# Transposes by DMA, row sums inside the value matmuls, and a reordered start, in a kernel of sparse attention and two dense layers

## The chip, the cores and the metric

The kernel runs on one core of one Trainium2 chip. The metric is the time of one execution on the device in microseconds (us). Engines: PE is the matmul engine, PEld its weight loads, DVE the vector engine, ACT the scalar engine, POOL the engine that issues the software DMA queue, SP the one that issues stores and, after the change, transposes.

## The reference, cut to what matters

```python
# q, k, v: (8 batches, 8 heads, 576, 64) fp32;  w_in: 512 x 2048, w_out: 2048 x 512
scores = (1/sqrt(64)) * q @ k.T
mask_local   = (rel >= 0) & (rel < 32)                 # heads 0..3, rel = pos_q - pos_k
mask_strided = (rel >= 0) & (pos_k % 32 == pos_q % 32) # heads 4..7
attn = softmax(where(mask, scores, -1e9));  o = attn @ v
x = o.transpose(0, 2, 1, 3).reshape(8 * 576, 512)
h = x @ w_in
g = where(h > 0, h, exp(min(h, 0)) - 1)
out = g @ w_out
```

Per core that is 8 batches of 4 pairs of heads (two strided, two local), and two dense layers of 4608 x 512 x 2048. The dense layers are most of the work. The inputs q and k have a standard deviation of 0.1, so all scores are near zero; this comes back in the first experiment.

## The kernel before: the parts that the change touches

All inputs come in by the software DMA queue, which casts fp32 to bf16 on the way. A score matmul wants the head dimension on the partitions, so q and k are transposed on PE, into PSUM, and copied back by DVE. A row sum comes from a matmul with a block of ones; sums and values of two heads are put side by side as two 64-column tiles.

```python
def load_str(src, b, name):                  # strided heads of q, k or v
    t = p_in.tile([RS, HG, NS * D], BF16, tag=name, name=name)
    nc.gpsimd.dma_start(out=t, in_=src[b, HG:2*HG].rearrange("h (p s) d -> p h (s d)", s=NS))
# load_batch(b): qs, ks, vs (strided), then ql, kl, vl (local), all on nc.gpsimd

def piece_T(P):                              # transposes of one pair of heads
    for nm, dst in (("q", P.qT[:, 0:S]), ("k", P.kT[:, PRE:PRE + S])):
        ps = p_a.tile([128, S], BF16, tag="a", name="tp")
        ... nc.tensor.transpose(ps[:, o:o + RS], src[...], identity[0:RS, 0:RS])   # 8, or 6
        nc.vector.tensor_copy(dst, ps)

def piece_O(P, u, pm):                       # half a pair: sums, values, division
    ... nc.tensor.matmul(s_ps[x*D:(x+1)*D, :], lhsT=ones, rhs=pm[:, x], ...)       # x = 0, 1
    ... nc.tensor.matmul(o_ps[x*D:(x+1)*D, o:o+RS], lhsT=batch_in[P.b]["vs"][...], ...)
    ln = Ln(s_ps); rc = Exp(-ln)             # ACT, 128 x 288 each
    ... nc.vector.tensor_mul(dst, o_ps, rc)  # DVE, 128 x 288

def l1(nb, m):                               # 4 matmuls of 512 columns, one hidden block
    hps = p_h.tile([128, CHUNK], F32, tag="h")
    for c in range(KC): nc.tensor.matmul(hps, lhsT=w_in_sb[:, cc, m*128:(m+1)*128], ...)
    e = Exp(hps)                             # ACT
    e1 = min(e, 1) - 1;  g = max(e1, hps)    # DVE, two operations

while done < PB:                             # all of batch 0's attention first
    run_piece(pieces[done], ...); done += 1
for nb in range(NCH):
    for m in range(MC):
        if nb > 0: l2(nb - 1, m)             # 4 matmuls of 512 columns
        run_piece(pieces[done]); done += 1   # the next batch's attention, T of it first
        l1(nb, m)
```

The softmax here doesn't subtract the row's maximum and nothing guards it: scores larger than these inputs give would overflow.

## Time and profile before

| | before |
|---|---|
| time, median of the first 3 runs (range) | 362.08 us (359.04 to 363.35) |
| span of the profiled run | 361.1 us |
| first layer-1 matmul | 36.32 us |
| PE waiting for strided q and k, in all | 22.0 us |

A table of waits has the waiting engine with tile and line, what released it, then the sum in us, how often, and the longest. These two rows of the kernel before are the 22.0 us:

```profile
PE tp L203 <- DMA qs<-in_q_dram: 18.4, 3, 9.4
PE tp L203 <- DMA ks<-in_k_dram: 3.6, 3, 1.4
```

Both are waits of the transposes for their input, three times each, the last of them at 62 us. In the prediction you will see them again as single holes, in a view where each line is a stretch of like instructions: start, busy time, engine, line, output and inputs, weight and moving shapes, count, and in brackets the idle time before it. Busy times there contain pipeline drain; what a piece costs is the distance between starts.

### The profile page before, as it was taken

The page shows a single profiled execution, that of the slowest core. Times are in us where ns is not written, and L with a number is a line of the kernel's source. Part 1 is how long each engine was busy: PE and PEld are TensorE (multiplying, and loading weights), DVE is VectorE, ACT ScalarE, POOL GpSimd, SP SyncE. Part 2 cuts the span into 40 slices and gives each one's busy share as a digit, 9 for nine tenths or more (in the row PEclk, how much of TensorE's full clock was granted, in tenths as well). Part 3 has the DMA queues.
Part 4 walks back from the last instruction along what each step waited for, and adds up shares of the span by engine and source line. Part 5 has one row for each costly group of instructions (what it writes and reads, how often), then busy time and mean ns, then how long its engine had stood idle before and what let it go on. Part 6 is the DMA issues. An engine that isn't in the chain of part 4 may idle for free.

```text
span 361.1 us, 6843 instructions
## 1 busy us (share of the span) xinstructions
PE 329.1 (91%) x2656; PEld 161.5 (45%) x2656; DVE 243.8 (68%) x501; ACT 194.3 (54%) x377; POOL 92.3 (26%) x120
## 2 busy tenths in 40 slices
PE   1851986999999999999999999999999999999995
PEld 1630443454544544445454454444444444444442
DVE  2640797787877877777878777776666666666610
ACT  1650575667566666666666666664444433543411
POOL 7952843958507214510620000000000000000000
PEclk9999999899999999999999999999999999999999
DMA  6999999999959965992960111010111110021122
GB/s 91 113 178 178 107 199 158 99 159 152 142 93 102 96 101 72 87 114 63 119 48 29 31 31 31 29 32 29 46 44 30 34 55 29 29 59 31 30 71 76
DMA packets 88321, 29.03 MB, mean 80 GB/s; under 512 B 72672, under 2 KB 83680, under 8 KB 88288
## 3 DMA queue, kind: packets, MB, share of 16 engines
q0 software_dynamic: 82432, 19.14, 61.7%
q1 hardware_dynamic: 5856, 9.44, 9.1%
q8 instruction: 21, 0.34, 0.4%
q14 instruction: 12, 0.10, 0.1%
HBM read 38.21 MB, written 9.44 MB: 132 GB/s over the span
## 4 chain that ended last, share of the span: by engine, by line
PE 73%; DMA 12%; ACT 6%; POOL 4%; issue 2%; DVE 2%; ACTq 0%
PE ops L382 32%; PE hps L347 30%; DMA vs<-in_v_dram 5%; DMA ks<-in_k_dram 5%; PE tp L211 3%; PE tp L203 2%; PE sc L243 2%; ACT e L251 2%; ACT osb L387 2%; DMA vl<-in_v_dram 2%; DVE pm L259 2%; PE s_ps L286 1%; ACT ln L297 1%; PE s_ps L270 1%; POOL kl L85 1%
## 5 line engine op out<-in xcount | busy, mean ns | idle before, releaser
L347 PE MATMUL hps<-xT,w_in_sb 128*128 128x512 bf16 x576 | 151.4, 386 | 0.2
L382 PE MATMUL ops<-w_out_sb,g 128*128 128x512 bf16 x576 | 145.4, 379 | 0.0
L352 ACT ACTIVATE he<-hps 128x512 f32<-128x512 f32 x144 | 85.8, 596 | 103.7 <-PE hps L347 103.0
L382 PEld LDWEIGHTS <-g 128*128 128x128 bf16 x576 | 56.4, 98 | 68.0
L347 PEld LDWEIGHTS <-w_in_sb 128*128 128x128 bf16 x576 | 50.8, 99 | 53.3 <-issue 2.1
L251 ACT ACTIVATE e<-sc 72x576 bf16<-72x576 f32 (+1 forms) x60 | 38.3, 639 | 17.4 <-PE sc L243 17.4
L297 ACT ACTIVATE ln<-s_ps 128x288 f32<-128x288 f32 x64 | 26.3, 411 | 16.9 <-PE s_ps L270 8.7
L387 ACT COPY osb<-ops 128x512 f32<-128x512 f32 x36 | 21.1, 586 | 20.0 <-PE ops L382 20.0
L76 POOL DMA_DIRECT2D ql<-in_q_dram x32 | 27.2, 855 | 18.0 <-PE tp L211 6.6
L299 ACT ACTIVATE rc<-ln 128x288 f32<-128x288 f32 x64 | 28.4, 443 | 2.0
L85 POOL DMA_DIRECT2D kl<-in_k_dram x32 | 23.7, 758 | 19.7 <-DMA ks<-in_k_dram 5.5
L203 PE MATMUL tp<-identity,qs 72*128 72x72 bf16 x128 | 7.9, 213 | 18.4 <-DMA qs<-in_q_dram 18.4
L304 DVE TENSOR_TENSOR xT<-o_ps,rc 128x288 bf16<-128x288 f32 x32 | 14.6, 456 | 8.3 <-ACT rc L299 7.9
L309 DVE TENSOR_TENSOR xT<-o_ps,rc 128x288 bf16<-128x288 f32 x32 | 14.6, 457 | 7.8 <-ACT rc L299 5.0
L253 DVE TENSOR_TENSOR pm<-e,mask_s 72x576 bf16<-72x576 bf16 x32 | 14.5, 452 | 3.8 <-ACT e L251 2.4
L259 DVE TENSOR_TENSOR pm<-e,mask_l 128x576 bf16<-128x576 bf16 x32 | 14.6, 457 | 2.5 <-ACT e L251 0.5
L203 PEld LDWEIGHTS <-qs 72*128 72x128 bf16 x128 | 5.8, 108 | 19.9 <-DMA qs<-in_q_dram 18.7
L67 POOL DMA_DIRECT2D vs<-in_v_dram x8 | 5.7, 710 | 31.9 <-PE sc L243 31.6
L96 POOL DMA_DIRECT2D vl<-in_v_dram x8 | 9.6, 1197 | 11.8 <-PE tp L203 11.4
L286 PE MATMUL s_ps<-pm,ones 128*64 128x288 bf16 x64 | 10.6, 322 | 1.6 <-DVE pm L259 0.9
L203 PE MATMUL tp<-identity,ks 72*128 72x72 bf16 x128 | 7.9, 214 | 3.9 <-DMA ks<-in_k_dram 3.6
L291 PE MATMUL o_ps<-pm,vl 128*64 128x96 bf16 x192 | 10.6, 215 | 0.7 <-DMA vl<-in_v_dram 0.7
(343 smaller groups left out, 338.5 us busy)
## 6 DMA issues: line engine op xcount, KB each, us to landing
out_dram<-osb SPq DMA_DIRECT2D x32, 144.0 KB
qs<-in_q_dram POOLq DMA_DIRECT2D x8, 288.0 KB, 5.9
ks<-in_k_dram POOLq DMA_DIRECT2D x8, 288.0 KB, 7.7
vs<-in_v_dram POOLq DMA_DIRECT2D x8, 288.0 KB, 7.9
ql<-in_q_dram POOLq DMA_DIRECT2D x32, 72.0 KB, 6.3
kl<-in_k_dram POOLq DMA_DIRECT2D x32, 72.0 KB, 4.2
vl<-in_v_dram POOLq DMA_DIRECT2D x8, 288.0 KB, 5.5
w_in_sb<-in_moe_w_in_dram POOLq DMA_DIRECT2D x4, 512.0 KB, 10.9
```

Source lines behind the costliest of these rows:

```text
L76: nc.gpsimd.dma_start(out=t[:, h // 2, :, h % 2, :], in_=q[b, h].rearrange("(p s) d -> p s d", s=NS))
L85: nc.gpsimd.dma_start(out=t[:, h // 2, :, h % 2, :], in_=src[b, h].rearrange("(t p) d -> p t d", p=LQ))
L203: nc.tensor.transpose(ps[:, o:o + RS], src[:, P.g0 + x, 2 * sp * D:2 * (sp + 1) * D], identity[0:RS, 0:RS])
L251: nc.scalar.activation(e[0:R], sc[0:R, :, 0:W], ACT.Exp, scale=scale)
L259: nc.vector.tensor_mul(pm, e, mb.unsqueeze(1).to_broadcast([128, 2, W]))
L297: nc.scalar.activation(ln, s_ps, ACT.Ln)
L299: nc.scalar.activation(rc, ln, ACT.Exp, scale=-1.0)
L304: nc.vector.tensor_mul(dst, o_ps.rearrange(pat, z=2, sp=2), rc.rearrange(pat, z=2, sp=2))
L347: nc.tensor.matmul(hps, lhsT=w_in_sb[:, cc, m * 128:(m + 1) * 128], rhs=xT[:, cc, nb * CHUNK:(nb + 1) * CHUNK], start=(c == 0), stop=(c == ...
L352: nc.scalar.activation(e, hps, ACT.Exp)
L382: nc.tensor.matmul(ops, lhsT=g[:, m, kk * 128:(kk + 1) * 128], rhs=w_out_sb[:, m, :], start=(m == 0), stop=(m == MC - 1))
L387: nc.scalar.copy(o_sb, ops)
```

## The change

The intent is to take the transposes and the separate row sums off PE, so that beside the dense layers only scores and values stay on it, and to start the dense layers earlier. Cut to its core:

```diff
+ def dma_T(b, which):                       # batches 2..7: all of q or k of a batch at once
+     nc.sync.dma_start_transpose(out=out_.rearrange("p (c n) -> p c n", n=n), in_=in_)
  def piece_O(b, hp, u, pm):                 # batches 3..7
-     s_ps by ones matmuls, o_ps by two 64-column tiles
+     for x, c, vt, mv in pv_terms(b, hp, u, pm):   # vt: 128 columns, values beside ones
+         nc.tensor.matmul(o[x][:, c], lhsT=vt, rhs=mv, ...)
-     ln = Ln(s_ps);  rc = Exp(-ln);  x = o_ps * rc                    # 128 partitions
+     ln[lo] = Ln(o[0][hi]);  ln[hi] = Ln(o[1][lo]);  rc = Exp(-ln)    # two halves
+     x_out(lo, o[0], rc);  x_out(hi, o[1], rc)
...
- t0["ql"] = load_qloc(0); t0["kl"] = load_kloc(k, 0, "kl")            # casting software queue
+ load_ql(0, nc.scalar, 0); load_kl(0, nc.sync, 0)                     # plain fp32
+ load_ql(0, nc.sync, 1);   load_kl(0, nc.scalar, 1)
+ cast_q(nc.vector, 0); cast_k(nc.scalar, 0); ...                      # bf16 by DVE and ACT
...
- def l1(nb, m):  4 matmuls of 512 columns
+ def l1(j, t):   8 matmuls of 256 columns, two hidden blocks
+ def l1_wide(j, t):                         # batch 0: four blocks of 256, a 4 KB PSUM tile
+     Exp and Relu on ACT, one DVE operation per 1024 columns
...
+ spins(26); ... f12 ...                     # filler matmuls between batch 0's pieces
+ for h in range(2):                         # layer 1 of tokens 0..511 ahead of batch 1
+     for j in range(2):
+         l1_wide(j, 4 * h)
+         if h: piece_T(1, 2 + j)            # batch 1 still transposes on PE
+         l1(j, 4 * h + 2); l1(j, 4 * h + 3)
...
+     at(st - (5 if b == 3 else 4), lambda b=b: Ts(b, "qs", "ks"))
+     at(st - (2 if b == 3 else 4), lambda b=b: Ts(b, "kl", "ql"))
...
+ def l2_last(j, kk): two halves, copied by ACT and DVE, stored by two queues
```

The bf16 tiles of local q and k, of the values that have ones beside them and of all transposed tensors exist twice, so one batch is loaded while another is used. In `at(n, ...)` the time n counts layer-1 groups; `st` is the step of a batch's first scores. Transposes stand 4 steps ahead of them; for batch 3 the strided two stand 5 ahead and the local two 2.

## The prediction

> **What bounds the kernel now.** I read the page first: the span, the busy line, the 40 slices.
>
> ```profile
> span 361.1 us, 6843 instructions
> PE 329.1 (91%) x2656; PEld 161.5 (45%) x2656; DVE 243.8 (68%) x501; ACT 194.3 (54%) x377; POOL 92.3 (26%) x120
> ...
> PE   1851986999999999999999999999999999999995
> ...
> DMA  6999999999959965992960111010111110021122
> ```
>
> PE is in the nines from slice 7 (about 62 us) to the end. Before that it has holes, and there the DMA row is full. So there are two stages: a start that waits for data, then a stage in which PE never rests. The windows view says so in numbers (columns: window, length, busy us of PE, PEld, DVE, ACT, POOL, clock, DMA share, GB/s):
>
> ```profile
> 20.00:30.00 10.00, 3.16 (x41) 2.02 (x41) 2.90 (x7) 4.03 (x10) 3.85 (x5) 1.00 1.23 202
> 30.00:40.00 10.00, 4.81 (x32) 2.22 (x33) 2.01 (x3) 1.13 (x2) 4.38 (x6) 1.00 2.27 141
> ...
> 100.00:150.00 50.00, 49.80 (x474) 24.55 (x471) 39.74 (x83) 33.85 (x68) 17.20 (x22) 1.00 0.85 94
> ```
>
> From 100 to 150 us PE is busy 49.8 of 50, DVE 39.7, ACT 33.9. The PE timeline of the start names the hole:
>
> ```profile
> 23.92 0.45 PE L291 MATMUL o_ps<-pm,vl 128*64 128x96 bf16 x6
> 33.78 0.66 PE L203 MATMUL tp<-identity,qs 72*128 72x72 bf16 x8 [9.42 <-DMA qs<-in_q_dram]
> 35.85 0.66 PE L203 MATMUL tp<-identity,ks 72*128 72x72 bf16 x8 [1.41 <-DMA ks<-in_k_dram]
> 36.32 1.90 PE L347 MATMUL hps<-xT,w_in_sb 128*128 128x512 bf16 x4
> ...
> 60.55 0.43 PE L203 MATMUL tp<-identity,qs 72*128 72x72 bf16 x8 [2.43 <-DMA qs<-in_q_dram]
> 61.80 0.66 PE L203 MATMUL tp<-identity,ks 72*128 72x72 bf16 x8 [0.82 <-DMA ks<-in_k_dram]
> 62.27 1.90 PE L347 MATMUL hps<-xT,w_in_sb 128*128 128x512 bf16 x4
> ```
>
> Batch 0's attention ends at 24.4 us; the first layer-1 matmuls start only at 36.3, because the program puts batch 1's transposes ahead of them. After 62.27 there is no hole.
>
> For the price of each piece I subtract start times in the steady PE timeline (its busy column includes pipeline drain):
>
> ```profile
> 150.36 0.31 PE L286 MATMUL s_ps<-pm,ones 128*64 128x288 bf16 x2
> 150.48 0.32 PE L291 MATMUL o_ps<-pm,vl 128*64 128x96 bf16 x6
> 150.73 0.43 PE L203 MATMUL tp<-identity,qs 72*128 72x72 bf16 x8
> 151.17 0.42 PE L203 MATMUL tp<-identity,ks 72*128 72x72 bf16 x8
> 151.43 1.03 PE L347 MATMUL hps<-xT,w_in_sb 128*128 128x512 bf16 x4
> 152.29 1.03 PE L382 MATMUL ops<-w_out_sb,g 128*128 128x512 bf16 x4
> 153.25 0.30 PE L243 MATMUL sc<-qT_95,kT_92 64*128 64x72 bf16 x8
> 153.49 1.04 PE L347 MATMUL hps<-xT,w_in_sb 128*128 128x512 bf16 x4
> ```
>
> The output piece (sums and values) is 150.73 - 150.36 = 0.37; the transposes 151.43 - 150.73 = 0.70, whose first eight take 0.44 and the next eight, of equal size, 0.26, so about 0.18 is a switch; four layer matmuls 0.86; the scores 0.24; and a layer-2 group that is followed by attention takes 0.96 rather than 0.86, so entering attention costs 0.10. One pair of heads is T + 2 S + 2 O + three entries = 0.70 + 0.48 + 0.75 + 0.30 = 2.23 us, 8.9 for a batch. The chain gives an independent count: equal places of two successive batches start 29.84 us apart (81.95, 111.79, 141.63); less 12 steps of 1.73 for the two layers that leaves 9.1. I use 9.1. PE's whole load is then 1152 layer matmuls x 0.216 = 249 plus 8 x 9.1 = 73, or 322 us; the other 39 us are the start and a tail of 4 us (the last output copy starts at 357.07).
>
> **What the Trainium skill says.** "TensorE: Matmul & The Clock Gate", under "Wait — 56ns, not 53.3ns?": a warm matmul of N columns costs N/2.4 ns plus about 2.5. The trace agrees: 0.865/4 = 216 ns at N = 512. For N = 256 that gives an estimate of 109 ns, so twice as many half-size layer-1 matmuls cost 576 x 2.5 ns = 1.4 us more. The same page, under "What you observe" and "What's actually happening", has an idle array fall to half clock: after the 9.4 us hole four matmuls took 1.90 instead of 1.03, so the trace agrees, and the filler matmuls of the change are meant for this. "SBUF — State Buffer", section "Door 1: The DMA port swizzle" (note on cachelines): 16-byte lines, full rate with two hits or more per line. The new layer-1 weights are read at a step of four bf16, 8 bytes, just two hits. No run here shows it yet. "DMA: Bandwidth & Descriptors", "Latency and other measured facts": a DMA transpose moves some 261 GB/s. A batch has 3 x 327,680 + 294,912 = 1.28 MB, an estimate of 5 us per batch, hidden if right; this trace has no such transfer.
>
> **The change part by part.**
>
> (1) Crossbar transposes for batches 2 to 7. Off PE go 24 pairs x 0.70 = 16.8 us, and 48 copies of 0.45 us off DVE.
>
> (2) For batches 3 to 7 the row sums come out of the value matmuls (ones beside the values as 128-column weights). O falls from 0.37 to 8 x 72 / 2400 = 0.24: 40 x 0.13 = 5.2 us. Without column tiling the entry into O should be nearly free too: some of 0.10 x 40, I take 2. My count per batch is 4 x (0.48 + 0.48 + 0.19) = 4.6 for batches 3 to 7, and 6.6 for batch 2, which keeps the old O and enters four times per pair: 4 x (0.48 + 0.76 + 0.40). PE load after: 249 + 1.4 + 2 x 9.1 + 6.6 + 5 x 4.6 = 298, that is 24 less.
>
> (3) DVE and ACT pay for (2): two half-partition multiplies and two logs in place of one each, 40 x 0.456 = 18 us on DVE and 40 x 0.411 = 16 on ACT. For batches 3 to 7 a batch has 16 layer-1 steps, 16 layer-2 steps and 4 pairs: 32 x 0.865 + 4.6 = 32.3 us of PE. DVE: 16 x (0.43 + 0.69) + 8 x 0.457 + 16 x 0.456 = 28.9. ACT: 16 x 0.596 + 8 x 0.64 + 16 x 0.411 + 8 x 0.443 + 4 x 0.586 = 27.1. Both stay below PE, at 89% and 84%.
>
> (4) The start. Batch 0's local q and k come as plain fp32 on the hardware queues and are cast by DVE and ACT; the software queue is left to the strided heads, v and w_in. Layer 1 of batch 0 now comes ahead of anything of batch 1. Two things must be ready: ACT has some 18 us of work for batch 0 (8 x 0.64 + 8 x 0.85, plus copies and casts), from about 5 us, so attention ends near 23; and w_in. Before, the same bytes had landed near 32 us. The transfers now start 3 to 4 us earlier, with q in 2 KB rows, so I put the first half of w_in at 24 and the second at 29. Layer 1 thus starts near 24 instead of 36.3. Later, w_out and batch 1 (before: landed near 57) bind: I expect 52 to 56, with PE waiting 3 to 8 us in all.
>
> (5) The end: the last outputs leave in half tiles on two engines and two queues: 4.1 us becomes about 3.5.
>
> Sum: 24 + (298 - 9 for batch 0) + 3.5 = 316.5 without a hole; with 3.5 us of waiting, **320 us**. Against 362 that is 12 us from the earlier start of layer 1, 24 from less PE work, and the rest small.
>
> **The rivals.**
>
> A. The start stays bound by transfers. For: its DMA row is full, and batch 1 and w_out still need the same bytes. Against: 16 layer-1 steps' worth of work needs only batch 0 and w_in. If batch 1 is complete only at 62, the time is near 328 to 332.
>
> B. Short strided weight loads are not hidden in layer 1. For: one load per 109 ns instead of per 216. Against: eight transposes with a weight load each took 0.26, or 33 ns a load. If 10 ns showed on each, 1152 x 10 ns = 12 us: 332.
>
> C. DVE or ACT becomes the bound at 85 to 90%, or crossbar transposes hold up the output stores on the same SP queue until three output buffers are full. For: the loads in (3). Against: four transposes at 5 us per 32 us, and buffers for three tiles. Either would add 5 to 20 us.
>
> D. The start runs better than I think (layer 1 at 20, no hole afterwards): 311.
>
> **Range and chances.** 320 lies between D and A/B; each single failure costs about 10, so 310 to 332 should hold it 8 times in 10. To lose the whole gain, two or three rivals would have to strike fully at once: faster by over 2% 0.97, within 2% 0.02, slower 0.01.
>
> **What the profile after would show.** Layer-1 groups of 8 x 256 columns 0.87 us apart (B false) or 0.95 and more; steady PE busy at 98% or more, DVE near 89% (C false); the first layer-1 matmul near 24 us; no PE hole over 3 us after 60; a batch from 3 on taking 32.3 us. The number is wrong if the first layer-1 matmul comes after 30, if batch 1's values land after 60, or if stores queue behind transposes.

## The result, and the profile after

| | before | after |
|---|---|---|
| median (range), 4 runs each | 362.61 us (359.04 to 363.35) | 320.18 us (319.83 to 321.01) |
| ratio (95% interval) | 1 | 0.884 (0.880 to 0.889) |

A ratio here can differ a little from the ratio of the medians (0.883 here). The prediction was right: 320.0 against 320.18.

The page of the changed kernel, in the rows that the prediction showed of the kernel before:

```profile
span 318.7 us, 7610 instructions
PE 304.9 (96%) x2857; PEld 221.9 (70%) x2900; DVE 237.7 (75%) x478; ACT 219.3 (69%) x428; POOL 121.9 (38%) x168
...
PE   8899999889999999999999999999999999999995
...
DMA  7999999999999999993999399949111111112112
```

PE is busy from the first slices on; the hole at the start is gone (some of it is fillers, so the timeline has to confirm it). The DMA row now stays full until slice 28: loads and transposes go on beside the matmuls. The windows of the changed kernel (window, length, busy us of PE, PEld, DVE, ACT, POOL, clock, DMA share, GB/s):

```profile
20.00:30.00 10.00, 9.87 (x104) 8.49 (x104) 4.89 (x10) 6.63 (x13) 4.49 (x8) 1.00 1.16 209
30.00:40.00 10.00, 9.94 (x113) 9.50 (x112) 9.14 (x17) 7.79 (x11) 4.79 (x6) 1.00 1.11 211
...
100.00:150.00 50.00, 49.45 (x459) 36.19 (x467) 43.88 (x89) 39.70 (x82) 28.73 (x38) 1.00 1.28 138
```

From 20 to 40 us PE works 19.8 of 20 us where it worked 8.0 before. In the steady stage it is still the fullest engine; DVE rose from 39.74 to 43.88 of 50 and ACT from 33.85 to 39.70. The PE timeline of the changed kernel's start:

```profile
23.57 1.48 PE L484 MATMUL idle<-warm 128*128 128x256 bf16 x12
24.89 1.91 PE L428 MATMUL hpw<-xT,w_in_sb 128*128 128x256 bf16 x16
26.63 1.91 PE L403 MATMUL hps<-xT,w_in_sb 128*128 128x256 bf16 x16
...
33.84 0.42 PE L267 MATMUL tp<-identity,qs 72*128 72x72 bf16 x8
...
38.55 1.92 PE L403 MATMUL hps<-xT,w_in_sb 128*128 128x256 bf16 x16
40.30 1.03 PE L460 MATMUL ops<-w_out_sb,g 128*128 128x512 bf16 x3
```

Twelve fillers bridge the last wait, layer 1 begins at 24.89, and its 16 matmuls of 256 columns take 26.63 - 24.89 = 1.74 us, which is the full rate. The transposes of batch 1 come in the middle of it, when their data have landed. The PE timeline of the steady stage:

```profile
154.29 1.04 PE L403 MATMUL hps<-xT,w_in_sb 128*128 128x256 bf16 x8
155.90 0.43 PE L290 MATMUL sc<-qsT,ksT 64*128 64x72 bf16 x16 [0.57 <-DMA ksT<-ks]
156.27 1.04 PE L460 MATMUL ops<-w_out_sb,g 128*128 128x512 bf16 x4
...
158.88 0.43 PE L342 MATMUL ox<-pm,vsx 72*128 72x72 bf16 x8
159.14 1.04 PE L403 MATMUL hps<-xT,w_in_sb 128*128 128x256 bf16 x8
```

There are no transposes and no separate sums any more. All 16 score matmuls of a pair stand together and take 0.37; a half pair's outputs take 159.14 - 158.88 = 0.26. The one wait is for a k that the DMA transposed: 0.57 us. The issue of transposes can be seen in SP's timeline (two successive batches):

```profile
116.08 1.36 SPq L164 DMA_TRANSPOSE qsT<-qs  x1
148.39 2.60 SPq L164 DMA_TRANSPOSE qsT<-qs  x1
```

The distance is 32.31 us, then 32.34 to the next one at 180.73 and 32.05 to the last at 212.78: that is about the time of one batch. On PE itself the first scores of batches 4 to 7 start at 123.52, 155.90, 187.64 and 219.59, so 32.38, 31.74 and 31.95 us apart.

### The profile page after: what moved, and what is told of

Read it like the earlier page. It is cut to its first block, busy times and chain, and to the rows that moved or that the text cites. A ratio compares the mean times of both kernels' runs of the same rounds, so it can differ in the third digit from the quotient of the medians.

```text
span 318.7 us, 7610 instructions
## 1 busy us (share of the span) xinstructions
PE 304.9 (96%) x2857; PEld 221.9 (70%) x2900; DVE 237.7 (75%) x478; ACT 219.3 (69%) x428; POOL 121.9 (38%) x168
## 4 chain that ended last, share of the span: by engine, by line
PE 83%; DMA 6%; DVE 3%; ACT 3%; issue 2%; SPq 1%; POOL 0%; DVEq 0%; ACTq 0%
PE ops L460 35%; PE hps L403 34%; DMA ksT<-ks 3%; PE sc L290 3%; PE ox L342 3%; DMA ks<-in_k_dram 3%; PE hpw L428 2%; PE idle L484 1%; PE opl L475 1%; PE tp L267 1%; DVE g L418 1%; ACT osb L465 1%; PE o_ps L375 1%; ACT rc L384 1%; SPq L164 1%
## 5 line engine op out<-in xcount | busy, mean ns | idle before, releaser
L403 PE MATMUL hps<-xT,w_in_sb 128*128 128x256 bf16 x1088 | 140.6, 273 | 0.7 <-DVE xT L314 0.4
L403 PEld LDWEIGHTS <-w_in_sb 128*128 128x128 bf16 x1088 | 117.5, 113 | 23.0 <-issue 0.8
L418 DVE TENSOR_TENSOR g<-he,hps 128x512 bf16<-128x512 bf16 x130 | 89.4, 687 | 13.9 <-PE hps L403 0.5
L417 DVE TENSOR_SCALAR he<-he 128x512 bf16<-128x512 f32 x130 | 58.4, 449 | 21.0 <-ACT he L410 19.6
L293 ACT ACTIVATE e<-sc 128x576 bf16<-128x576 f32 (+1 forms) x64 | 38.5, 646 | 5.9 <-PE sc L290 5.8
L114 POOL DMA_DIRECT2D qlb<-in_q_dram x28 | 23.3, 838 | 16.6 <-DMA ks<-in_k_dram 7.9
L120 POOL DMA_DIRECT2D klb<-in_k_dram x28 | 21.5, 776 | 11.6 <-DMA w_in_sb<-in_moe_w_in_dram 5.5
L128 POOL DMA_DIRECT2D vlx<-in_v_dram x28 | 22.1, 789 | 6.8 <-DMA klb<-in_k_dram 2.7
L345 ACT ACTIVATE ln<-ox 64x288 f32<-64x288 f32 x40 | 16.3, 408 | 10.5 <-PE ox L342 10.0
L314 DVE TENSOR_TENSOR xT<-ox,rc 64x288 bf16<-64x288 f32 x40 | 18.1, 453 | 5.6 <-ACT rc L348 5.4
L310 DVE TENSOR_TENSOR xT<-ox,rc 64x288 bf16<-64x288 f32 x40 | 18.1, 454 | 5.3 <-ACT rc L348 5.0
L129 POOL DMA_DIRECT2D vlx<-in_v_dram x28 | 17.5, 624 | 1.3 <-DMA klb<-in_k_dram 0.6
L346 ACT ACTIVATE ln<-ox 64x288 f32<-64x288 f32 x40 | 16.1, 403 | 0.5
```

The costliest lines, as they stand in the source:

```text
L114: nc.gpsimd.dma_start(out=qlb[b % 2][0:RS, h // 2, :, (h % 2) * D:(h % 2 + 1) * D], in_=q[b, h].rearrange("(p s) d -> p s d", s=NS))
L120: nc.gpsimd.dma_start(out=klb[b % 2][:, h // 2, :, (h % 2) * D:(h % 2 + 1) * D], in_=k[b, h].rearrange("(t p) d -> p t d", p=LQ))
L128: nc.gpsimd.dma_start(out=t[PRE:128], in_=x)
L293: nc.scalar.activation(e[0:R], sc[0:R, :, 0:W], ACT.Exp, scale=scale)
L310: nc.vector.tensor_mul(xs[:, u * W:(u + 1) * W], o[pr], rc[pr])
L314: nc.vector.tensor_mul(dst, o[pr].rearrange(pat, b=3, s=NS), rc[pr].rearrange(pat, b=3, s=NS))
```

## The experiments

Twelve kernels were run, in three groups, each beside runs of the kernel before; its medians in these groups were 361.66, 361.11 and 362.70 us. All results passed the comparison with the reference. Unless it is said otherwise, an experiment is the changed kernel with one edit, and "costs" is the median minus 320.18. The changed kernel was not run again in these groups, and the kernel before moved by 1.6 us between them, so a cost is good to about 1 us. The question is whether the parts of the prediction's sum are worth what it gave them. Part (5), the end, has no run of its own.

### The transposes: three tries to put them back on PE

**First try.** The transposes of every pair go back to PE, one step ahead of its scores.

```diff
- at(st - (5 if b == 3 else 4), lambda b=b: Ts(b, "qs", "ks"))
- at(st - (2 if b == 3 else 4), lambda b=b: Ts(b, "kl", "ql"))
+ at(SC[b][i] - (.5 if b == 2 else 1), lambda b=b, p=p: piece_T(b, p, (nc.vector, nc.scalar)))
```

> The changed kernel with batches 2 to 7 transposed on PE again (copies shared by DVE and ACT), everything else as changed. Theory (PE bounds the stage after the start): the 24 pairs bring back 24 x 0.52 to 0.70 us of PE, less some 3 us of PE holes that waited for the crossbar: 320 becomes 330 to 337. Rival (the gain comes from the start; the transposes off PE were worth little because DVE and ACT bound the stage at 85 to 90%): 318 to 324.

Measured: 381.79 us (380.86 to 383.26), ratio 1.055. This is a failed experiment, for two reasons. One is in its waits:

```profile
PE sc L290 <- ACT klT L254: 17.6, 12, 1.6
```

One step is too short a lead for the copies: PE stood still for ACT's copies of k, 17.6 us for local heads and about as much again for strided ones. The other reason is a mistake of mine: the loads of batch 3 and later stand ahead of the transposes of the batch before in program order, so some PE transposes of strided heads read the next batch's q and k (the tiles of the local heads exist twice). The comparison passed all the same. The likely reason is that scores this near to zero give almost equal weights whatever q and k are, so this comparison does not guard q and k well. The run prices nothing.

**Second try.** Transposes three steps ahead (one and a half for batch 2), and batch 3's loads after batch 2's transposes, so that the data are right.

```diff
+ at(SC[b][i] - (1.5 if b == 2 else 3), lambda b=b, p=p: piece_T(b, p, (nc.vector, nc.scalar)))
- if b > 3: at(st - 13, loads of batch b)
+ at(st - 13 if b > 3 else 6.5, loads of batch b)
```

> The first attempt at undoing the crossbar transposes put PE's transposes one step before the scores that need them, and PE waited some 1.6 us per pair for the copy out of PSUM; it also let batch 3's strided q and k be loaded before batch 2's were transposed. Here the transposes stand 3 steps ahead (1.5 for batch 2) and batch 3's loads come after batch 2's transposes. Theory (PE bounds, price of the transposes 0.52 us plus an entry of 0.1 each, 24 pairs, less some 3 us of waits for the crossbar): 331 to 337. Rival (transposes off PE are worth little): 318 to 324.

Measured: 361.54 us (361.2 to 362.67), ratio 0.9997. It costs 41 us, as much as the whole change, which cannot be the PE time of 24 pairs. The window of this run, and a stretch of its PE timeline:

```profile
150.00:200.00 50.00, 43.92 (x452) 32.20 (x458) 36.88 (x77) 34.01 (x70) 24.00 (x33) 1.00 0.90 88
```

```profile
173.62 0.42 PE L342 MATMUL ox<-pm,vlx 128*128 128x96 bf16 x6 [0.53 <-ACT ksT L254]
```

PE is busy 43.92 of 50: it is waiting, not working. The wait named is that of an output matmul for the copy of transposed k, on which its data do not depend. What ties them is the PSUM tile: scores, outputs and these wide transposes share a pool of two double tiles (4 KB per partition). An output must wait until a transpose has been copied out, and the other way round.

**Third try.** q and k are transposed one step apart, each through one single tile (2 KB) of layer 1's pool of three.

```diff
+ def half_T(b, hp, nm, eng):
+     ps = p_h.tile([128, S], BF16, tag="h", name="tp")
+     ... nc.tensor.transpose(ps[:, j*n:(j+1)*n], x, identity[0:n, 0:n]);  copy(eng, dst, ps)
+ at(SC[b][i] - (1.5 if b == 2 else 3), half_T(b, p, "q", nc.vector))
+ at(SC[b][i] - (1 if b == 2 else 2),   half_T(b, p, "k", nc.scalar))
```

> Transposes on PE again, ahead as in the second attempt (361.5 us), but q and k one step apart, each through one of the three single PSUM banks that layer 1 uses, in place of one of the two double banks that scores and outputs share. If the second attempt's 41 us (against some 14 of PE time) came from five tenants for two double banks: 333 to 345. If they came from the copies' share of DVE and ACT or their latency: 352 to 365.

Measured: 334.65 us (333.76 to 335.65), ratio 0.923 (0.920 to 0.927). It costs 14.5 us. The PE timeline of this run:

```profile
150.25 0.42 PE L276 MATMUL tp<-identity,qlb 72*128 72x72 bf16 x8
150.51 1.03 PE L468 MATMUL ops<-w_out_sb,g 128*128 128x512 bf16 x4
152.76 0.42 PE L276 MATMUL tp<-identity,klb 96*128 96x96 bf16 x6
153.01 1.03 PE L468 MATMUL ops<-w_out_sb,g 128*128 128x512 bf16 x4
```

From 150 to 200 us PE now never rests (50.00 of 50), and the eight and the six transposes take 0.26 and 0.25 us from start to start. That is 24 x 0.51 = 12.2 us, and the measured 14.5 is a little more (entering the transposes is not in the 0.51). So taking the transposes off PE is worth about 14.5 us, and 41 was the price of an undo that crowded PSUM. (The third try also puts q and k a step apart; what that alone brings was not tried.)

### The row sums

Batches 3 to 7 take their sums from separate matmuls again, as batch 2 does; ln, rc and the multiply are whole again.

```diff
- do(("X" if b == 2 else "O", b, p, u))
+ do(("X", b, p, u))
```

> The changed kernel with batches 3 to 7 using the former output piece: column-tiled ones for the row sums, separate value matmuls, one log and one full-width multiply. PE gets 40 x (0.13 + about 0.05) us more, DVE 18 and ACT 16 us less. Theory (PE bounds): 325 to 328. Rival (DVE and ACT, at 88 and 80% between 100 and 200 us, already cost PE as much through waits as the merging saves): 317 to 322.

Measured: 328.60 us (328.12 to 329.38), ratio 0.908. It costs 8.4 us, just above the range that I expected. The window of this run:

```profile
150.00:200.00 50.00, 50.00 (x479) 34.15 (x478) 36.49 (x72) 33.62 (x66) 23.35 (x31) 1.00 1.08 133
```

DVE falls from 43.10 (changed kernel, same window) to 36.49 and ACT from 39.29 to 33.62, and the kernel is slower all the same, since PE is full. The rival that DVE's and ACT's added work eats the gain is refuted.

### Is PE the bound? A known load on PE alone

Five filler matmuls of 256 columns go ahead of 24 of the layer-1 groups, by the prediction's rate 24 x 5 x 0.109 = 13.1 us of PE and of nothing else.

```diff
+ for _ in range(pad): spin(hps[:, 0])
+ l1(j, t, mode=..., pad=5 if n < 96 and n % 4 == 1 else 0)
```

> The changed kernel with five filler matmuls of 256 columns ahead of 24 layer-1 groups (every fourth step for 96 steps), into the bank that the group then starts anew: 24 x 5 x 0.109 = 13.1 us more of PE and nothing else, no copy, no PSUM slot, no work for DVE or ACT. That is the bare PE price of the transposes (24 x 0.52 us). If PE bounds this stage: 330 to 334. If PE only seems busy and DVE, ACT or the PSUM slots set the pace: 320 to 326.

Measured: 332.20 us (331.28 to 332.57), ratio 0.916. Of 13.1 us added, 12.0 show in the time. The missing 1.1 fits the waits for transposed k: they sum to 1.0 us in the changed kernel, and this run's trace has none of them. PE bounds the stage. This is the direct reason that work taken off PE counts nearly in full.

### The start

**Layer 1 after batch 1's transposes.** Two transpose pieces of batch 1 are moved ahead of layer 1; in the kernel before, too, layer 1 stood behind transposes of batch 1.

```diff
+ piece_T(1, 2)
+ piece_T(1, 3)
  for h in range(2):
      for j in range(2):
          l1_wide(j, 4 * h)
-         if h: piece_T(1, 2 + j)
```

> The changed kernel with the strided transposes of batch 1 put ahead of batch 0's layer 1, as the kernel before had it: layer 1 then starts near 33 us instead of 24.9. Theory (an early layer 1 is worth its whole lead): 8 us later, some 1 us of later waits gained back, 1.7 us for a cold array: 326 to 330. Rival (the start is bound by the transfers of batch 1 and w_out, and PE would only wait later): 319 to 323.

Measured: 328.92 us (327.47 to 329.5), ratio 0.907. It costs 8.7 us. Its PE timeline:

```profile
31.24 0.66 PE L267 MATMUL tp<-identity,qs 72*128 72x72 bf16 x8 [5.65 <-DMA qs<-in_q_dram]
...
34.71 3.20 PE L428 MATMUL hpw<-xT,w_in_sb 128*128 128x256 bf16 x16
```

The hole of the kernel before is back (5.65 us here, 9.42 there), layer 1 starts 9.8 us later than in the changed kernel, and 8.7 of them reach the end. Its first 16 matmuls take 3.20 us instead of 1.91 after the pause.

**The order alone, in the kernel before.** Here the edit is to the kernel before: layer 1 of the first 512 tokens goes ahead of batch 1's transposes, and w_out ahead of batch 1's values and local heads (two changes at once, so that w_out is there in time).

```diff
+ for m in range(MC): l1(0, m)
+ for i in range(PB): l2(0, i); run_piece(pieces[done], lag=1); done += 1
- for nb in range(NCH):
+ for nb in range(1, NCH):
```

> The kernel before with one part of the change alone: batch 0's layer 1 ahead of anything of batch 1, batch 1's attention beside layer 2 of the first block, and w_out loaded ahead of batch 1's v and local heads. Transposes, sums, loads and block size stay as before. Theory (an earlier layer 1 is worth about its lead): 347 to 353 against 361.7. Rival (the start is bound by transfers): 358 to 363.

Measured: 361.43 us (360.47 to 361.7), ratio 0.997 (0.994 to 0.999). My expectation was wrong: I expected 12 us or so of gain and got 1.3. The rival's number was right, but its reason, that transfers bind, was not. The PE timeline of this run:

```profile
23.92 3.08 PE L353 MATMUL hps<-xT,w_in_sb 128*128 128x512 bf16 x8
...
36.69 2.08 PE L353 MATMUL hps<-xT,w_in_sb 128*128 128x512 bf16 x8 [0.81 <-DVE g L362]
39.59 2.08 PE L353 MATMUL hps<-xT,w_in_sb 128*128 128x512 bf16 x8 [0.81 <-DVE g L362]
```

Three rows of its waits, over the whole run:

```profile
PE hps L353 <- DVE g L362: 6.0, 9, 1.0
PE s_ps L292 <- DVE pm L265: 5.2, 7, 1.2
PE s_ps L276 <- DVE pm L259: 3.9, 7, 1.0
```

Layer 1 does start 12.4 us earlier. But with nothing between its groups, two groups take 39.59 - 36.69 = 2.90 us, 1.45 for one, against 0.86 of PE work: PE waits for DVE to finish g and give back one of only two PSUM tiles. The 16 groups end near 47.3 instead of near 38. Nor is that all: from 48 to 107 us PE stands still for another 9.6 us, 7.7 of them for pm, DVE's masked attention weights. Layer 2 of the first block has been brought forward, and from about 79 us the attention of the next batches stands beside layer 1 alone. In sum the new order moved PE's idle time and did not remove it: 16.4 us after 24 us here, 17.0 in the kernel before. In the changed kernel the same work runs at full rate (24.89 to 40.30, with four transpose sets in it), with wide groups that need one DVE operation per 1024 columns and with three single PSUM tiles. In the kernel before, the earlier start is worth little without a layer 1 that can keep its pace and without work to put beside the attention that follows; which of the wide groups, the third tile and the later order matters most was not tried.

**Without the fillers.** Each run of filler matmuls is cut to one.

```diff
- for _ in range(n):
+ for _ in range(min(n, 1)):
      spin(idle)
```

> The changed kernel without its filler matmuls (one is left). Theory: the array is at half clock through batch 0's attention and for the first 3 to 4 us of layer 1: 322 to 325. Rival (ACT and DVE carry batch 0's attention, so a slow array costs nothing before layer 1, and its first microseconds hide): 319.5 to 321.

Measured: 323.22 us (322.88 to 324.04), ratio 0.893. They are worth 3.0 us: without them the attention of batch 0 runs slower on PE (two sum matmuls near 21 us take 0.45 instead of 0.31), and 15 of the first 16 layer-1 matmuls start at 26.22 and take 3.36 us.

**Local q and k of batch 0 by the casting software queue**, as before the change.

```diff
- load_ql(0, nc.scalar, 0); load_kl(0, nc.sync, 0); load_ql(0, nc.sync, 1); load_kl(0, nc.scalar, 1)
+ load_ql16(0); load_kl16(0)
```

> The changed kernel with batch 0's local q and k loaded by the casting software queue, as before, in place of plain fp32 on the hardware queues with casts on DVE and ACT. Eight more issues of 0.8 us stand ahead of the strided heads, v and w_in on that queue, so batch 0's attention and w_in come 4 to 6 us later. Theory: layer 1 starts near 29 to 31 us instead of 24.9 and the time is 324 to 327. Rival (attention of batch 0 is bound by ACT from its own start and w_in has slack): 320 to 322.

Measured: 324.62 us (323.88 to 327.76), ratio 0.900. The hardware queues are worth 4.4 us. (In its profiled run, the slowest of the four, layer 1 starts at 31.89.)

### How well are the DMA transposes hidden?

**Every transpose issued twice**, to the same target, so the result is unchanged.

```diff
+ for _ in range(2):
      nc.sync.dma_start_transpose(...)
```

> The changed kernel with every crossbar transpose issued twice, some 8 us more of transfers a batch on the queue that also carries the output stores. Theory (they are hidden but arrive late at a batch's start already): PE waits longer at each batch, 321 to 326. Rival (the transposes are on the path, stores pile up behind them): over 330.

Measured: 386.60 us (384.75 to 388.63), ratio 1.067. Wrong again: I expected the second copy to be hidden. The longest of its PE waits:

```profile
PE sc L291 <- DMA ksT<-ks: 40.8, 6, 8.8
```

With another 12.4 us for local q, PE waits 53 us for transposed tensors, and its clock falls with the holes (mean 0.87 from 150 to 200 us). The run doubles more than the bytes: a second copy to the same target waits for the first to land (SP's queue spends 81 us waiting for transposes), so it doubles the latency as well, and SP's stores queue behind. In the changed kernel the transposes are thus hidden, but by a lead of few microseconds, not by a wide margin. How much is bytes and how much latency stays open.

**Transposes of batches 4 to 7 issued 7 steps ahead instead of 4.**

```diff
- at(st - (5 if b == 3 else 4), ...);  at(st - (2 if b == 3 else 4), ...)
+ at(st - (5 if b == 3 else 7), ...);  at(st - (2 if b == 3 else 7), ...)
```

> The changed kernel with the crossbar transposes of batches 4 to 7 issued 7 steps ahead of their scores in place of 4. In the changed kernel PE waits 0.57 us and more for the transposed k at the start of a batch. If those waits are real loss on PE: 316.5 to 319.5. If PE's slack is elsewhere, or the output stores behind the transposes suffer: 320 to 322.

Measured: 319.38 us (319.34 to 319.6), ratio 0.8835 (0.880 to 0.887), against 0.8841 (0.880 to 0.889) of the changed kernel. The two are not told apart. It is the lowest time seen, no proven gain, and fits a changed kernel that loses only 1.0 us to such waits.

### Three undone at once

The second try of the transposes, the separate sums and the later layer 1 together.

> Three parts undone together: transposes on PE (ahead), separate sums for batches 3 to 7, batch 1's transposes ahead of layer 1. If PE's time simply adds up, the sum of the three single differences to the changed kernel: 8.4 (sums) + 8.7 (late layer 1) + 11 to 17 (transposes) over 320.2, so 348 to 354; what is then missing to 361.7 belongs to fillers (3) and the rest. If the parts share a hidden bound (transfers, DVE or ACT), clearly less than the sum: under 343.

Measured: 361.49 us (360.16 to 362.63), ratio 0.9997. It was to show whether the parts add up, but it contains the crowding of PSUM of the second try, so it says nothing on that.

## Why the prediction was right, point by point

- **The bound.** PE was named as the bound and is: at least 49.45 of 50 us in the steady stage (eight matmul records are missing in it), and 12.0 of 13.1 us of padding show.
- **Start (4).** Layer 1 was put near 24 and started at 24.89. The two halves of w_in were put at 24 and 29; issued at 9.6 and 10.4, they landed 13.8 and 19.4 us later, near 23.4 and 29.8. Putting layer 1 back behind the transposes costs 8.7 us, and the prediction gave the earlier start 12. Its reading was right for this kernel but told half of it: the run on the kernel before shows that order alone brings 1.3. By that run's waits, a layer 1 that keeps its pace and work beside the attention after it belong to this gain, and the prediction never priced them.
- **Transposes (1).** Predicted 24 x 0.70 = 16.8, measured 14.5. The 0.70 holds an 0.18 switch, read where transposes follow outputs in two column tiles. In the changed kernel the outputs are not tiled so, and putting transposes back costs 0.51 plus an entry.
- **Row sums (2).** Predicted 5.2 + 2 = 7.2, measured 8.4.
- **PE load.** Predicted 289 us after 24 (298 less batch 0), and 3.5 of holes. Measured from 24.89 to the last matmul's end at 314.80: 289.9 with the holes. The windows leave PE idle for 6.6 us between 20 and 300 us, but that is not all waiting. 41 matmul records are missing there (2533 on PE, 2574 weight loads), and most of the idle times are of 0.05 to 0.16 us beside a group that is a record short. The waits after 24 us that have a named cause sum to 3.5: 1.0 for transposed k and 2.5 for DVE. So the holes were as predicted, and the load is about 286, which is 3 less than predicted. The 3 are in the scores: 16 together take 0.37, not 0.48, and enter once per pair, so a batch costs 4 x (0.37 + 0.10 + 2 x 0.26) = 4.0 instead of 4.6, or 3 us over five batches. The hit to 0.2 us has luck in it all the same: layer 1 began 0.9 later, the tail was 0.4 longer, and the 1.7 us between span and time were left out, which cancels these 3. The mechanism is what was right.
- **Period.** Predicted 32.3 us a batch; on PE 32.38, 31.74 and 31.95. Here too the parts differ: 31.7 is 32 layer groups and an attention of 4.0, and the 32.38 has a hole of 0.57 in it.
- **DVE and ACT (3).** Predicted 89% and 84%, measured 88% and 79%. Neither binds, as the run with separate sums showed; that half of rival C is refuted.
- **Rival B**, unhidden weight loads: refuted. Eight matmuls of 256 columns take 302.47 to 303.34 = 0.87 us. A load itself became longer, 113 ns against 99 in the costliest groups, but stays hidden; whether that comes from the step of the weights was not tested. This also agrees with the note on cachelines in the Trainium skill that the prediction drew on ("SBUF — State Buffer", section "Door 1: The DMA port swizzle"): a step of 8 bytes, two hits to a line, costs the matmuls no rate.
- **Rival A**, a start bound by transfers: no PE hole is over 0.6 us after 25. The prediction also counted 3 to 8 us of waiting, with w_out and batch 1's loads as the cause. The amount is right (3.5 us, 2.6 of them between 40 and 80), the cause is not: of these 2.6 the trace gives 2.2 to DVE (masked attention weights and x) and 0.4 to a transposed k, none to w_out or to a load of batch 1.
- **The other half of rival C**, transposes in the way: 1.0 us of waits for k. But the estimate behind it was too low. For a batch, 5 us were predicted and 7.9 to 12.0 measured (batches 4 to 7), and the run that issues each twice shows the lead to be thin.
- **Tail (5).** Predicted 3.5 us, measured 318.7 - 314.80 = 3.9; before 4.1. Beside the tail of the kernel before, halving the last outputs brought next to nothing; no run undoes it alone.

The costs of the single undos are 14.5 + 8.4 + 8.7 + 3.0 + 4.4 = 39.0, near the 42.4 us between the medians. (From the ratios they are 14.2, 8.5, 8.3, 3.2 and 5.6.) That they add up is not shown; three of them touch the same start.

## What to carry to other kernels

Price a piece on a full engine by the distance between starts, including what entering and leaving it costs in that neighbourhood, and ask whether a start that comes earlier can also keep its pace: here an earlier layer 1 was worth 1.3 us where it then waited for one of two PSUM tiles and the attention after it had lost the matmuls beside it. Before you call idle time of PE a wait, look whether records are missing there. Undo a change only with the lead and the PSUM tiles that the restored work needs, or the undo measures itself (381.8 and 361.5 us, where 334.7 was the answer). When a transfer takes over work, measure its lead by doubling it: "no wait seen" and "a wide margin" are different things.

## What the Trainium skill lacked or had wrong

- "DMA: Bandwidth & Descriptors", "Latency and other measured facts", gives one kernel's DMA transposes as 261 GB/s. Here, beside other transfers and with pauses included, the transposing packets of a batch (1.28 MB) took 10.3, 11.3, 12.0 and 7.9 us in batches 4 to 7, or 107 to 163 GB/s. The page gives no time from the issue of a transpose to its landing: one issued at 148.39 let its source be overwritten at 153.90, 5.5 us later.
- What issuing a transpose costs the issuing queue stands in no page as a time on this chip; the same page has only cycle counts of "previous generations", in its section on trn3. SP was occupied 1.3 to 4.8 us by each, median 1.6 to 2.0, and stores wait behind.
- "TensorEngine Tiling (Array Packing)", "Key Properties", says that a change of tiling mode drains the engine, without a size. Eight transposes after outputs in two column tiles took 0.44 us and the next eight 0.26, so 0.18 for the switch; entering attention from the dense layers cost 0.10. That draining is the reason was not isolated by a run.
